# Column sums of the key features from one operand of 128 partitions: two products instead of four, moved behind the first down tile

## The chip, the cores and the metric

One core of a Trainium2 chip runs the whole program. Its engines work side by side and wait for each other by semaphores: TensorE (PE, matrix products into PSUM), VectorE (DVE), ScalarE (ACT), GpSimd (POOL) and SyncE (SP), whose queue issues nearly all DMAs. Each engine runs its instructions in the order in which they stand in the program. The metric is the time of one execution on the device in microseconds; lower is better. Three runs of the kernel before took 445.38, 446.20 and 446.23 us, the median is 446.2.

## What is computed

`x` is 2048 rows of 512. Part A is a linear attention with 32 heads of 16 columns, part B a dense layer with Mish, and a gate mixes them row by row:

```python
g = _sigmoid((x * gate_w).sum(-1, keepdims=True))
# A: q, k, v of x @ wqkv, by head
phi_q = concat(softmax(q @ w_phi), softmax(-(q @ w_phi)))
phi_k = concat(softmax(k @ w_phi), softmax(-(k @ w_phi)))
kv  = einsum("bhsf,bhsd->bhfd", phi_k, v)
z   = einsum("bhsf->bhf", phi_k)            # sums over all 2048 rows
o   = einsum("bhqf,bhfd->bhqd", phi_q, kv) / (einsum("bhqf,bhf->bhq", phi_q, z) + 1e-6)
a   = o @ wo
b   = mish(x @ w1 + b1) @ w2
out = g * a + (1 - g) * b
```

The change is about `z`: for each of 2 x 512 feature columns one sum over all rows, which is needed on every partition, since every row of `phi_q` is multiplied with it.

## The kernel before

The kernel runs in two parts. Part A goes over eight chunks of 256 rows, two tiles of 128 rows each. For a tile it makes the products for k, v and q, turns k into its two softmaxes (maximum and minimum by head, two subtractions, exponential, sums `S`, reciprocal `rS`, and the scaling `ml`), stores q to DRAM for later (`st`), and adds the tile's features to `zacc` on GpSimd (`z0`, `z1`; L324, 128 partitions by 1024 columns). At the end of every second chunk `kv` multiplies features and v into one PSUM bank. After the last chunk `km` masks and turns that bank, and eight small DMAs put it into `kvb`.

Part B goes over four blocks of 512 rows. A block has eleven `up` tiles (`up0` to `up10`, 12 products with w1 each, called U0, U1, ... in the prediction), each followed by `mi` (Mish on ScalarE), `hi` (its high half, ScalarE), `lo` (the rest, GpSimd), and eleven `dn` (down) steps, each with the products of one such tile with w2 into four PSUM banks. `gr` (ScalarE and SP, L560) copies the one row of `up0` that holds the gate's argument out of PSUM, sends it to DRAM, and reads it back by rows. `hc` and `cd` deal with a leftover of the first tile. In between the attention of the block is worked off: `lq` loads q again, `mx`, `mn`, `d0`, `d1`, `E`, `S`, `rS` make its features as in part A, `T` multiplies them with the sums `zb`, `D`, `m`, `de`, `rd` and `sc` make the divisor, `es` scales, `tr` transposes on VectorE and stores to DRAM (`ed`), `mv` reads it back turned (`eT`), `nu` multiplies it with `kvb` (`num`), `oh` and `ol` split the result, `wo` multiplies with wo, and `fi` stores the output. The numeral behind a step is its tile; a `+` behind it means the next block's, a `'` the previous chunk's.

Every float32 product is made from parts: a value is split into a high part in a reduced format (`float32r`) and the rest, and three products (high by high, high by rest, rest by high) are added. So is `z`: `zh` (L459) makes the high part of `zacc` on ScalarE, `zl` (L485) the rest on VectorE, and `z` (L476) multiplies a matrix of ones with both, for each half of the columns: four products. A product with ones sums over the 128 partitions and leaves the sum on all of them. Two activations bring the results into `zb`.

The order of all steps is written out by hand in the texts FIRST to BLOCK. Each word runs the function of that name, and every instruction is pinned, so that each engine keeps the order of the text; what the engines do at the same time follows from their waits. LAST is the last chunk of part A, BLOCK0 the first block of part B.

PSUM has eight banks: three take turns for the `up` tiles and for the k and q products of part A (tag `a`), four for the v products and the down sums (tag `dn`), and one is for `kvp` (tag `kv`), later used by `num` and `wo`. A tile that takes a bank over has to wait until the last reader of the tile before it is done. In SBUF two buffers of 1024 columns (tag `tx`) hold x of a chunk as loaded, then the parts of `zacc`, then `T`. wo is loaded in two pieces (`ldo0`, `ldo1`); `WH0` and `WH1` make their high parts on ScalarE, `WL0` and `WL1` the rest on GpSimd (L446).

Almost all matrix products are recorded on L100 and all activations on L120, which are helpers; the tile's name tells them apart.

Of the kernel before, what the change touches and what calls it, by code (L numbers as in the profile page):

```python
# [9 lines left out]
F32R = mybir.dt.float32r  # L10
# [42 lines left out]
"""  # L53
LAST = """
    k0 mx0 mn0 d00 d10 k1 E0 XH0 mx1 mn1 d01 d11 wx E1 v0 S0 rS0 ml0 z0 ve0 XH1 S1 rS1 ml1 z1 XL0 XL1
    v1 ve1 lq2+ mx1+ mn1+ d01+ d11+ q0 qe0 st0 q1 zh qe1 st1 E1+ zl kv' kv S0+ rS0+ km
"""

BLOCK0 = """
    up0 mi0 hi0 lo0 gr lq3 ldo0 ldo1 S1 rS1 mx2 mn2 up1 @z mi1 hi1 lo1 hc T0 D0 m0 de0 rd0 sc0 es0 tr0 up2 mi2 hi2 lo2 dn0
    T1 D1 m1 de1 rd1 sc1 es1 tr1 mv0 lq0+ lq1+ d02 d12 mx3 mn3 d03 d13 up3 mi3 hi3 lo3 WH0 dn1
    up4 mi4 hi4 lo4 WH1 WL0 dn2 E2 S2 T2 rS2 D2 m2 de2 rd2 sc2 es2 tr2 up5 mi5 hi5 lo5 WL1 dn3 E3 ge gg up6 mi6 hi6 lo6 dn4
    up7 mi7 hi7 lo7 dn5 S3 T3 rS3 D3 m3 de3 rd3 sc3 es3 tr3 mv1 up8 mi8 hi8 lo8 dn6
    mx0+ mn0+ d00+ d10+ mx1+ mn1+ d01+ d11+ lq2+ lq3+ up9 mi9 hi9 lo9 dn7 E0+ E1+ S0+ T0+ LX0 rS0+ D0+ m0+ de0+ rd0+ sc0+
    up10 mi10 hi10 lo10 dn8 dn9 cd nu0 nu1 oh0 ol0 es0+ tr0+ XH0+ XL0+ S1+ T1+ rS1+ LX1 df0 df1 wo0 ag0 wo1 oh1 ol1 ag1 D1+ fi0
    m1+ de1+ rd1+ sc1+ df2 df3 wo2 ag2 fi1 XH1+ XL1+ es1+ fi2 wo3 ag3 fi3 tr1+ mv0+
"""
# [19 lines left out]
def tile_gated_mix(ctx: ExitStack, tc: tile.TileContext, xT, wv, wkT, wqT, bd, w1a, w1b, b1, w2a, w2b, wo, out):  # L89
# [6 lines left out]
    pin = tc.keep_in_program_order  # L96
    V, G_, A_, Sy = nc.vector, nc.gpsimd, nc.scalar, nc.sync

    def mm(*a, **k):
        return pin(nc.tensor.matmul(*a, **k))  # L100

    def T(shape, dt, tag, bufs, name):
        nm[0] += 1
        return sp.tile(shape, dt, name=f"{name}_{nm[0]}", tag=tag, bufs=bufs)
# [4 lines left out]
    def k4(name, tag, dt=F32):  # L109
        return T([P, 1024], dt, tag, {"tx": 2, "oh": 2, "z": 1}[tag], name)  # L110

    def k2(name, tag, dt=F32):
        return T([P, 512], dt, tag, {"pq": 3, "io": 4, "hl": 8}[tag], name)

    def psum(name, tag, bufs={"a": 3, "dn": 4, "kv": 1}):
        nm[0] += 1
        return pp.tile([P, 512], F32, name=f"{name}_{nm[0]}", tag=tag, bufs=bufs[tag])

    def act(out_, in_, fn=AF.Copy, **k):
        return pin(A_.activation(out_, in_, fn, **k))  # L120
# [7 lines left out]
    def f32(ap):  # L128
        return ap.bitcast(F32)
# [48 lines left out]
    onr = T([P, P], F32R, "hc", 1, "onr")  # L178
# [20 lines left out]
    def at(key, name, fn):  # L199
        steps.setdefault((key, name), []).append(fn)  # L200
# [12 lines left out]
    zacc = k4("zacc", "z")  # L213
# [240 lines left out]
    B = {}  # L454

    def mid_ops():
        key = ("A", NCH - 1)

        def zh():  # L459
            B["zs"] = [k4("zs", "tx", F32R) for _ in range(2)]  # L460
            act(B["zs"][0], zacc)

        def km():

            B["km"] = k2("km", "io")
            m = B["km"][:, :256]
            pin(V.tensor_mul(m.rearrange("p (n x) -> p n x", x=32), kvs[0].rearrange("p g (a x) -> p (g a) x", a=2), mask[:, None, :].to_broadcast([P, 8, 32])))
            pin(V.transpose(m, m))
            m = m.rearrange("p (g a x) -> p g a x", g=NG, a=2)
            for e in range(2):  # L470
                for r in range(2):
                    for a in range(2):
                        o, i = 64 * r + 32 * a, 64 * e + 32 * r
                        pin(Sy.dma_start(kvb[o : o + 32, e::2, :], m[i : i + 32, :, a, :]))

        def z():  # L476
            B["zb"] = k4("zb", "z")
            for a in range(2):
                ps = psum("z", "dn")
                for j in range(2):  # L480
                    mm(ps, onr, B["zs"][j][:, a * 512 : (a + 1) * 512], start=(j == 0), stop=(j == 1))
                act(B["zb"][:, a * 512 : (a + 1) * 512], ps)

        at(key, "zh", zh)
        at(key, "zl", lambda: pin(V.tensor_sub(B["zs"][1], zacc, f32(B["zs"][0]))))  # L485
        at(key, "km", km)
        at(("B", 0), "@z", z)


# [219 lines left out]
    wo_ops()  # L709
    w2_ops(("A", NCH - 1))  # L710
    mid_ops()
    for b in range(NB):
        b_ops(b)
# [155 lines left out]
```

## Time and profile before

| | |
|---|---|
| median of three runs | 446.2 us (445.38 to 446.23) |
| the profiled execution | 445.59 us |
| its span, first to last instruction | 443.7 us |
| granted TensorE clock, mean | 1.000 |
| part A on TensorE | up to about 149.8 us of the span |
| first block of part B | from about 149.8 us on |

The profile is of one execution. Its times count from the start of the span, and the 1.9 us between 443.7 and 445.59 lie around it. In a row of a timeline stand the start, the duration, the engine, the line, the operation, the tiles written and read, their shapes, how many instructions are merged in the row, and in brackets how long the engine was idle before and who released it. A duration of a TensorE row is longer than the time until the next one starts, as products overlap; the distance of starts counts. Rows of waits have the engine that waits, who releases it, the sum, the number of waits and the longest one. Rows of DMA issues have tiles, the queue, how many, the KB of each and the median time to landing.

### The profile page before, as it was taken

Reading aid. Unit: us, or ns where it says so; the run is one execution under the profiler, and the core shown is the slowest. Engines: PE = TensorE matmul, PEld = TensorE weight load, DVE = VectorE, ACT = ScalarE, POOL = GpSimd, SP = SyncE. Lnnn points to the kernel's source line nnn. Section 1 sums busy time; section 2 is a strip of 40 time slices with the busy share of each in tenths; the row PEclk is TensorE's granted clock in tenths of the full one; section 3 lists DMA queues with packets and bytes.
Section 4 is the critical chain, followed back from the end, with each engine's and each line's share of the span. In section 5 each row is a group of like instructions: output and inputs, shape, how many; then the busy total and the mean of one; then the engine's idle time right before and its main releaser. Section 6 shows DMA issues by size and latency. Waiting matters only on the chain.

```text
span 443.7 us, 7192 instructions
## 1 busy us (share of the span) xinstructions
PE 439.0 (99%) x2878; PEld 360.5 (81%) x2878; DVE 310.0 (70%) x414; ACT 203.8 (46%) x290; POOL 160.9 (36%) x100
## 2 busy tenths in 40 slices
PE   8999999999999999999999999999999999999997
PEld 7888888888888888887888878888878888887885
DVE  3987658459399999999999898369679329601103
ACT  3644433444335384836366442646352645342331
POOL 3078686676862344621023120214310222411121
PEclk9999999999999999999999999999999999999999
DMA  7721622614504126326353524322505302320002
GB/s 264 283 96 47 193 79 87 193 13 176 189 27 120 49 46 220 103 97 189 120 195 113 148 95 139 94 96 95 191 0 184 102 1 95 118 72 1 1 0 95
DMA packets 28809, 49.11 MB, mean 111 GB/s; under 512 B 6244, under 2 KB 14948, under 8 KB 28776
## 3 DMA queue, kind: packets, MB, share of 16 engines
q1 hardware_dynamic: 28456, 48.26, 33.6%
q8 instruction: 22, 0.36, 0.4%
q10 hardware_dynamic: 288, 0.39, 0.3%
q14 instruction: 11, 0.09, 0.1%
q0 software_dynamic: 32, 0.01, 0.0%
HBM read 31.21 MB, written 16.79 MB: 108 GB/s over the span
## 4 chain that ended last, share of the span: by engine, by line
PE 98%; DMA 1%; SPq 0%; DVE 0%; issue 0%
PE proj L100 30%; PE up L100 27%; PE down L100 26%; PE wo L100 10%; PE kvp L100 2%; PE num L100 2%; DMA wT<-in_wkT_dram 1%; PE fuse L100 1%; PE rest L100 0%; PE z L100 0%; DVE io L687 0%; SPq L156 0%; SPq L148 0%
## 5 line engine op out<-in xcount | busy, mean ns | idle before, releaser
L521 POOL TENSOR_TENSOR l<-act,h 128x512 fp32r<-128x512 f32 (+1 forms) x44 | 63.4, 1442 | 217.4 <-ACT h L120 190.8
L120 ACT ACTIVATE act<-up,b1s 128x512 f32<-128x512 f32 x44 | 30.3, 688 | 78.2 <-PE up L100 77.8
L324 POOL TENSOR_TENSOR zacc<-zacc,E 128x1024 f32<-128x1024 f32 x16 | 39.7, 2484 | 38.6 <-DVE E L286 38.6
L120 ACT ACTIVATE E<-E 128x1024 f32<-128x1024 f32 x32 | 33.6, 1061 | 41.5 <-DVE E L271 41.5
L286 DVE TENSOR_TENSOR E<-E,Sm 128x1024 f32<-128x1024 f32 x32 | 46.1, 1442 | 1.0
L100 PE MATMUL wo<-woh,ohl 128*128 128x512 f32 x128 | 41.2, 389 | 0.0
L275 DVE TENSOR_REDUCE Sm<-E 128x64 f32<-128x1024 f32 x32 | 38.5, 1204 | 0.0
L100 PE MATMUL down<-w2ah,h 128*128 128x512 f32 x96 | 37.6, 392 | 0.0
L256 DVE TENSOR_REDUCE mx<-proj 128x32 f32<-128x512 f32 x16 | 11.0, 690 | 31.4 <-PE proj L100 31.4
L100 PE MATMUL down<-w2al,h 128*128 128x512 f32 x80 | 31.2, 390 | 0.0
L100 PE MATMUL down<-w2ah,l 128*128 128x512 f32 x80 | 31.1, 389 | 0.0
L120 ACT ACTIVATE h<-act 128x512 fp32r<-128x512 f32 (+2 forms) x48 | 30.3, 632 | 1.5
L422 DVE TENSOR_TENSOR xbl<-xraw,xbh 128x1024 fp32r<-128x1024 f32 x8 | 12.0, 1528 | 26.8 <-ACT xbh L120 26.8
L100 PE MATMUL down<-w2bh,h 128*128 128x512 f32 x78 | 30.6, 392 | 0.0
L100 PE MATMUL down<-w2bl,h 128*128 128x512 f32 x78 | 30.4, 389 | 0.0
L100 PE MATMUL down<-w2bh,l 128*128 128x512 f32 x78 | 30.4, 389 | 0.0
L100 PEld LDWEIGHTS wo<-woh,ohl 128*128 128x128 f32 x128 | 24.0, 188 | 5.0
L120 ACT ACTIVATE io<-wo,g_sb 128x512 f32<-128x512 f32 x16 | 11.0, 690 | 36.1 <-PE wo L100 36.1
L120 ACT ACT_TABLE_LOAD x19 | 24.4, 1283 | 3.5 <-PE up L100 3.2
L100 PE MATMUL up<-xbh,w1ah 128*128 128x512 f32 x96 | 25.8, 390 | 0.0
L100 PE MATMUL up<-xbh,w1al 128*128 128x512 f32 x96 | 25.7, 389 | 0.0
L100 PE MATMUL up<-xbl,w1ah 128*128 128x512 f32 x96 | 25.7, 389 | 0.0
(126 smaller groups left out, 977.5 us busy)
## 6 DMA issues: line engine op xcount, KB each, us to landing
ed<-E SPq DMA_DIRECT2D x16, 512.0 KB, 2.9
eT<-ed SPq DMA_DIRECT2D x64, 128.0 KB, 3.3
xraw<-in_xT_dram SPq DMA_DIRECT2D x15, 512.0 KB, 5.0
pqd<-qs SPq DMA_DIRECT2D x16, 256.0 KB, 2.7
pq<-pqd SPq DMA_DIRECT2D x16, 256.0 KB, 3.9
out_dram<-io SPq DMA_DIRECT2D x15, 256.0 KB, 2.0
raw<-in_w1a_dram SPq DMA_DIRECT2D x3, 512.0 KB, 5.5
raw<-in_w2a_dram SPq DMA_DIRECT2D x3, 512.0 KB, 4.1
```

Of the source, the lines that this page charges most:

```text
L100: return pin(nc.tensor.matmul(*a, **k))
L120: return pin(A_.activation(out_, in_, fn, **k))
L256: pin(V.tensor_reduce(d[name], hv(src()), axis=AX.X, op=op))
L275: pin(V.tensor_reduce(d["S"], hv(d["E"][:, :]), axis=AX.X, op=ALU.add))
L286: pin(eng.tensor_mul(hv(d["E"][:, :]), hv(d["E"][:, :]), d["S"][:, :, None].to_broadcast([P, 2 * H, DH])))
L324: at(key, f"z{t}", lambda d=d: pin(G_.tensor_add(zacc, zacc, d["E"])))
L422: pin(V.tensor_sub(xb[b][1][:, :, sl], kt(raw[h], SC), f32(xb[b][0][:, :, sl])))
L521: pin(G_.tensor_sub(U[i]["l"][:n, :], U[i]["a"][:n, :], f32(U[i]["h"][:n, :])))
```

## The change

`z` is made otherwise. The upper 64 partitions of `zacc` are copied to the lower ones by a DMA (`zd`), GpSimd adds the two halves (`zf`), and the high part (`zh`, now 64 partitions) and the rest (`zl`, written to the upper 64 partitions) stand in one tile `zs` of 128 partitions. So one product with ones adds both parts and all partitions, two products in all. `zd` and `zf` stand in LAST where `zh` and `zl` were; these two are now in BLOCK0, `zh` ahead of `gr` and `zl` behind `S1 rS1`. `z` itself moves behind `dn0`, which in turn has `up2` and `up3` ahead of it, and its results are in the banks of the tags `kv` and `a` instead of `dn`. Some steps of the attention in BLOCK0 (`d02 d12 mx3`) go ahead of `T0`, and `WL0` and `WL1` move back behind `lo8` and `lo9`.

```diff
 LAST = """
...
-    v1 ve1 lq2+ mx1+ mn1+ d01+ d11+ q0 qe0 st0 q1 zh qe1 st1 E1+ zl kv' kv S0+ rS0+ km
+    v1 ve1 lq2+ mx1+ mn1+ d01+ d11+ q0 qe0 st0 q1 zd qe1 st1 E1+ zf kv' kv S0+ rS0+ km
 """
...
 BLOCK0 = """
-    up0 mi0 hi0 lo0 gr lq3 ldo0 ldo1 S1 rS1 mx2 mn2 up1 @z mi1 hi1 lo1 hc T0 D0 m0 de0 rd0 sc0 es0 tr0 up2 mi2 hi2 lo2 dn0
-    T1 D1 m1 de1 rd1 sc1 es1 tr1 mv0 lq0+ lq1+ d02 d12 mx3 mn3 d03 d13 up3 mi3 hi3 lo3 WH0 dn1
-    up4 mi4 hi4 lo4 WH1 WL0 dn2 E2 S2 T2 rS2 D2 m2 de2 rd2 sc2 es2 tr2 up5 mi5 hi5 lo5 WL1 dn3 E3 ge gg up6 mi6 hi6 lo6 dn4
-    up7 mi7 hi7 lo7 dn5 S3 T3 rS3 D3 m3 de3 rd3 sc3 es3 tr3 mv1 up8 mi8 hi8 lo8 dn6
-    mx0+ mn0+ d00+ d10+ mx1+ mn1+ d01+ d11+ lq2+ lq3+ up9 mi9 hi9 lo9 dn7 E0+ E1+ S0+ T0+ LX0 rS0+ D0+ m0+ de0+ rd0+ sc0+
+    up0 mi0 hi0 lo0 @zh gr lq3 ldo0 ldo1 S1 rS1 @zl mx2 mn2 up1 mi1 hi1 lo1 d02 d12 mx3 up2 mi2 hi2 up3 dn0 @z hc lo2 mi3 hi3 lo3
+    T0 D0 m0 de0 rd0 sc0 es0 tr0 T1 D1 m1 de1 rd1 sc1 es1 tr1 mv0 lq0+ lq1+ mn3 d03 d13 WH0 dn1
+    up4 mi4 hi4 lo4 WH1 dn2 E2 S2 T2 rS2 D2 m2 de2 rd2 sc2 es2 tr2 up5 mi5 hi5 lo5 dn3 E3 ge gg up6 mi6 hi6 lo6 dn4
+    up7 mi7 hi7 lo7 dn5 S3 T3 rS3 D3 m3 de3 rd3 sc3 es3 tr3 mv1 up8 mi8 hi8 lo8 WL0 dn6
+    mx0+ mn0+ d00+ d10+ mx1+ mn1+ d01+ d11+ lq2+ lq3+ up9 mi9 hi9 lo9 WL1 dn7 E0+ E1+ S0+ T0+ LX0 rS0+ D0+ m0+ de0+ rd0+ sc0+
...
+        def zd():
+            B["zt"] = k4("zt", "tx")
+            pin(Sy.dma_start(B["zt"][:64, :], zacc[64:, :]))
+
         def zh():
-            B["zs"] = [k4("zs", "tx", F32R) for _ in range(2)]
-            act(B["zs"][0], zacc)
+            B["zs"] = k4("zs", "tx", F32R)
+            act(B["zs"][:64, :], zacc[:64, :])
...
             for a in range(2):
-                ps = psum("z", "dn")
-                for j in range(2):
-                    mm(ps, onr, B["zs"][j][:, a * 512 : (a + 1) * 512], start=(j == 0), stop=(j == 1))
+                ps = psum("z", ("kv", "a")[a])
+                mm(ps, onr, B["zs"][:, a * 512 : (a + 1) * 512], start=True, stop=True)
                 act(B["zb"][:, a * 512 : (a + 1) * 512], ps)
...
-        at(key, "zh", zh)
-        at(key, "zl", lambda: pin(V.tensor_sub(B["zs"][1], zacc, f32(B["zs"][0]))))
+        at(key, "zd", zd)
+        at(key, "zf", lambda: pin(G_.tensor_add(zacc[:64, :], zacc[:64, :], B["zt"][:64, :])))
+        at(("B", 0), "@zh", zh)
+        at(("B", 0), "@zl", lambda: pin(V.tensor_sub(B["zs"][64:, :], zacc[:64, :], f32(B["zs"][:64, :]))))
```

## The prediction

> **What bounds the kernel now.** Read first were the page's busy times, its chain of work and TensorE's own waits.
>
> ```profile
> span 443.7 us, 7192 instructions
> PE 439.0 (99%) x2878; PEld 360.5 (81%) x2878; DVE 310.0 (70%) x414; ACT 203.8 (46%) x290; POOL 160.9 (36%) x100
> ...
> PE 98%; DMA 1%; SPq 0%; DVE 0%; issue 0%
> ```
>
> ```profile
> PE warm L100 <- DVE ones L170: 1.1, 1, 1.1
> PE fuse L100 <- DMA bds<-in_bd_dram: 0.3, 1, 0.3
> PE fuse L100 <- DMA wT<-in_wkT_dram: 0.2, 1, 0.2
> ```
>
> TensorE is busy for 439.0 of 443.7 us, the chain is 98% TensorE, and these three rows, all from the start, are every wait that it has. So the other engines are hidden with some slack each, a product removed is worth its own time, and a wait put on TensorE is paid in full: nothing behind it gives it back. The edit lies at the step from part A to part B, so its timeline on TensorE came next.
>
> ```profile
> 149.79 1.20 PE L100 MATMUL up<-xbh,w1ah 128*128 128x512 f32 x4
> ...
> 152.64 1.07 PE L100 MATMUL up<-xbh,w1ah 128*128 128x512 f32 x4
> ...
> 155.36 1.07 PE L100 MATMUL z<-zs,onr 128*128 128x512 f32 x4
> 156.27 1.07 PE L100 MATMUL up<-xbh,w1ah 128*128 128x512 f32 x4
> ```
>
> These are the first tiles of products with w1, U0 to U2 (U3, the fourth, comes behind the first down products): each of 12 products takes 2.72 us (152.64 to 155.36), the four z products 0.91 us (155.36 to 156.27).
>
> **What is removed.** Two of four z products: 0.91 / 2 = 0.45 us off TensorE. That is all the change can win there, 0.10% of 446.2 us. The full-width zs on ScalarE and its remainder on VectorE go too; neither is on TensorE's path.
>
> **What is moved on TensorE: the price of the change.** The order becomes U0, U1, U2, U3, dn0, z, dn1. With neither z nor dn0 ahead of it, U3 could start two tiles after U1's start: 152.64 + 2 x 2.72 = 158.08. But U tiles take turns in three PSUM buffers (tag "a"), and in the built program U3 gets U0's. It must wait for ScalarE to have read U0 twice: mish, and gr, which copies the gate's row. gr is now behind zs on ScalarE, in a strict order.
>
> ```profile
> 149.62 1.06 ACT L120 ACTIVATE zs<-zacc 128x1024 fp32r<-128x1024 f32 x1 [3.71 <-POOL zacc L324]
> ...
> 153.09 1.06 ACT L120 ACTIVATE E<-E 128x1024 f32<-128x1024 f32 x1 [1.93 <-DVE E L271]
> 154.17 1.28 ACT L120 ACT_TABLE_LOAD   x1
> 155.47 0.69 ACT L120 ACTIVATE act<-up,b1s 128x512 f32<-128x512 f32 x1
> 156.19 1.29 ACT L120 ACTIVATE h<-act 96x512 fp32r<-96x512 f32 x2
> 157.50 0.63 ACT L120 ACTIVATE l<-act 32x512 fp32r<-32x512 f32 x1
> 158.15 0.59 ACT L120 ACTIVATE gr<-up 1x512 f32<-1x512 f32 x1
> 158.76 1.09 ACT L120 ACTIVATE zb<-z 128x512 f32<-128x512 f32 x2
> ```
>
> ScalarE's chain starts at 153.09 with the exponential, whose releaser is VectorE, and runs gapless through the table load to gr. Before, gr ended at 158.74, and z, U2 and dn0 kept TensorE busy until U3. Now zs starts where gr did, 158.15. Its price at 64 partitions is in no row; the bounds are 0.63 (half of its elements, like l) and 1.06 (as before). Rows of 96 and of 32 partitions take the same 0.63 to 0.65 (two in 1.29, one in 0.63), so partitions don't count and I take 1.06. gr then runs from 159.23 to 159.82. U3 is held from 158.08 to 159.82, 1.74, with the handing over about 1.8 us; with the lower bound 1.3.
>
> **What is added, and what hides it.** zd copies zacc's upper 64 partitions to the lower ones (256 KB); GpSimd adds them (zf); zs and its remainder (zl) make one 128-partition operand.
>
> ```profile
> 142.72 2.40 POOL L324 TENSOR_TENSOR zacc<-zacc,E 128x1024 f32<-128x1024 f32 x1 [8.80 <-DVE E L286]
> 146.37 3.22 POOL L324 TENSOR_TENSOR zacc<-zacc,E 128x1024 f32<-128x1024 f32 x1 [1.25 <-DVE E L286]
> 156.89 1.29 POOL L521 TENSOR_TENSOR l<-act,h 96x512 fp32r<-96x512 f32 x1 [7.31 <-ACT h L120]
> ```
>
> zacc is whole at 146.37 + 3.22 = 149.59; zd can go then. Behind it on SP wait only the store of the last q tile, read in the last block, and the copies to kvb, not due before 155. zf costs between 1.29 (512 elements) and 2.40 (1024); it has 1024, so 2.40. GpSimd was idle for 7.31 us before 156.89, so zf is hidden if the copy lands by 154.5. zl (1.21 at most) is due when z starts, after dn0 at 159.9 + 2.72 + 1.81 = 164.4, with zs done at 159.2: covered by 4 us. z's two results go to the kv buffer, read by km's mask before 156.2, and to U1's, free by then.
>
> ```profile
> w2x<-w2ah SPq DMA_DIRECT2D x1, 192.0 KB, 3.1
> w2al<-w2al SPq DMA_DIRECT2D x3, 64.0 KB, 2.0
> ```
>
> ```profile
> pqd<-qs SPq DMA_DIRECT2D x1, 256.0 KB, 2.0
> ```
>
> zd's landing is the one cost that matters and no row has it. Copies within SBUF of 64 and 192 KB take 2.0 and 3.1 us: 256 KB on that line 3.7. A store of 256 KB to DRAM took 2.0 between 150 and 152 (third row), so the bounds are 2.0 and 3.7. I take about 3.2, nearer to copies of its own kind: landing 152.8. The Trainium skill's "SBUF — State Buffer", section "Door 1: The DMA port swizzle", says that 64 partitions reach no more DMA ports than 32, half of what 128 reach. By its 196 to 218 GB/s the data would take an estimated 1.2 to 1.3 us instead of 0.6; the trace agrees in kind, as the 32-partition copy takes 2.0 with a quarter of the store's bytes.
>
> wo's two subtractions on GpSimd go from behind the fifth and sixth lo to behind the ninth and tenth, about 195 and 200. The first wo product comes at 210.97: 8 us of cover. hc and the fourth tile's mish move behind zb, about 165; that tile's down products come after U4 and dn2.
>
> ```profile
> 159.88 1.23 DVE L589 TENSOR_TENSOR T<-E,zb 128x1024 f32<-128x1024 f32 x1 [0.40 <-ACT zb L120]
> ...
> 173.10 0.72 DVE L269 TENSOR_TENSOR E<-pq,mx 128x512 f32<-128x512 f32 x1
> 173.74 2.88 DVE L271 TENSOR_TENSOR E<-mn,pq 128x512 f32<-128x512 f32 x1
> 176.55 0.67 DVE L256 TENSOR_REDUCE mx<-pq 128x32 f32<-128x512 f32 x1
> ...
> 196.01 1.25 DVE L604 STREAM_TRANSPOSE E<-E 128x1024 f32<-128x1024 f32 x1
> ```
>
> What else is late is VectorE's chain behind zb. T, at 159.88 before, now stands behind d02, d12 and mx3. zb ends about 166.0 (164.4 + 0.45 + 1.09); mx3 needs the fourth q tile:
>
> ```profile
> 163.75 0.49 SPq L585 DMA_DIRECT2D pq<-pqd  x1
> ...
> 197.69 4.29 SPq L627 DMA_DIRECT2D eT<-ed  x8
> ```
>
> ```profile
> pq<-pqd SPq DMA_DIRECT2D x16, 256.0 KB, 3.9
> ```
>
> km comes 1.1 earlier without the old zl, so this load is issued at 162.6, lands at 166.5, and T starts at 167.2: 7.3 late. The three moved operations, 173.10 to 177.14 before, give back 4.0. The fourth tile's transpose (196.01) is 3.3 late.
>
> ```profile
> 207.57 1.96 PE L100 MATMUL num<-eT,kvb 64*32 64x256 f32 x64
> DMA to landing us min/median/max: 2.6/3.3/6.0
> ```
>
> The last eT copy is issued at 201.98 + 3.3 = 205.3 and lands, at the median 3.3, at 208.6. Its half of num stood at 207.57 + 0.98 = 208.55 and comes 1.35 later, 209.9. So 1.3 us of slack is left: I cost it at nothing, at the maximum 6.0 it is 1.4 us.
>
> **The sum.** -0.45 + 1.8 = +1.35 us. On the profiled execution (443.7 span, 445.59 in all) that is 446.9, on the median of the runs shown (446.2) 447.6. The profiled one and the three runs (445.38 to 446.23) have the mean 445.85; from there it is 447.2, which I forecast.
>
> **Rivals.** (a) GpSimd gets in ahead of VectorE: slower.
>
> ```profile
> 151.78 0.67 DVE L269 TENSOR_TENSOR E<-pq,mx 128x512 f32<-128x512 f32 x1
> 152.38 0.68 DVE L271 TENSOR_TENSOR E<-mn,pq 128x512 f32<-128x512 f32 x1
> ```
>
> ```profile
> 130.99 2.93 POOL L324 TENSOR_TENSOR zacc<-zacc,E 128x1024 f32<-128x1024 f32 x1
> ```
>
> ```profile
> 130.99 0.67 DVE L269 TENSOR_TENSOR E<-pq,mx 128x512 f32<-128x512 f32 x1
> 131.59 2.88 DVE L271 TENSOR_TENSOR E<-mn,pq 128x512 f32<-128x512 f32 x1
> ```
>
> At 131 a GpSimd sum that came during d0 ran between d0 and d1, and d1 took 2.88 instead of 0.68. The same pair stands at 151.78 and 152.38, and its d1 releases the exponential that starts ScalarE's chain. If zf is ready before 152.38, that is, if zd lands within 2.7 us of 149.6, everything down to gr slips by 2.2 and the wait becomes 4.0: 445.85 - 0.45 + 4.0 = 449.4. The store's 2.0 speaks for it, the two copies' line against. By the Trainium skill's "DMA: Bandwidth & Descriptors", section "Anatomy of one DMA — SWDGE (gpsimd) path", a DMA takes 2.0 us plus its bytes at 436 GB/s, here an estimated 2.6, just on this side; the page gives it for GpSimd's own queue, and zd goes through SP's.
>
> (b) The eT landing of 6.0, or a wo subtraction holding one of the fourth tile's VectorE operations for its 2.4 us, uses up the 1.3 us: +1.4 on the forecast, 448.6.
>
> ```profile
> 146.12 4.54 DVE L422 TENSOR_TENSOR xbl<-xraw,xbh 128x1024 fp32r<-128x1024 f32 x2
> ```
>
> (c) Not slower: VectorE's two xbl subtractions, 4.54 together because the zacc of 146.37 ran between them, both go ahead of it. Then d1, and ScalarE's chain, come about 2.1 earlier, gr ends at 157.7, ahead of 158.08, and only -0.45 is left: 445.4. From 1.74 earlier on there is no wait. Against it: nothing ahead of 149.6 changes order on either engine.
>
> **How the numbers follow.** Forecast 0.62, (a) 0.17, (b) 0.14, (c) 0.05, anything else 0.02. The forecast's own range is 446.4 (zs at 0.63, the profiled base) to 447.7 (median base). With (b) and most of (a) it is 446.4 to 449.7. About 0.2% (0.9 us) can be told from no change; a gain of that size is out of reach at 0.45, so faster has 0.02. Same takes (c) and the low end of the forecast: 0.11. Slower 0.87.
>
> **What would show it.** Right: one new wait of TensorE, up on ScalarE's gr, of 1.8 us with U3 starting near 159.9; zs between l and gr; zf starting at about 153, after VectorE's d1 of 0.68. For (a): d1 stretched to about 2.9, U3 near 162. For (b): a num or down product waiting on a DMA near 210. Wrong: no wait at U3, or a landing of zd past 155.7, where zs itself would be late.

## The result and the profile after

The changed kernel takes 448.02 us (median of 6 executions, 447.78 to 449.56), the kernel before beside it 445.86 (445.38 to 446.36): a ratio of 1.0054, 95% interval 1.0039 to 1.0068. It is slower by 2.2 us; the forecast was 447.2 and a loss of 1.35 on the profiled execution. The profiled execution of the changed kernel took 447.78 with a span of 446.1 (before: 445.59 and 443.7), with the granted clock at 1.0 in both.

TensorE's waits in the changed kernel (total us, times, longest):

```profile
PE up L100 <- ACT gr L120: 1.6, 1, 1.6
PE warm L100 <- DVE ones L170: 1.1, 1, 1.1
PE fuse L100 <- DMA bds<-in_bd_dram: 0.4, 1, 0.4
PE fuse L100 <- DMA wT<-in_wkT_dram: 0.2, 1, 0.2
PE down L100 <- POOL l L527: 0.2, 1, 0.2
```

Two rows are new: the first, which was forecast, and the last, which was not. Their places on TensorE's timeline (start, length, what ran, and in brackets the idle time before it and its releaser):

```profile
149.69 1.20 PE L100 MATMUL up<-xbh,w1ah 128*128 128x512 f32 x4
...
159.77 1.19 PE L100 MATMUL up<-xbh,w1ah 128*128 128x512 f32 x4 [1.62 <-ACT gr L120]
...
162.63 0.39 PE L100 MATMUL down<-w2ah,h 128*128 128x512 f32 x1
...
164.44 0.61 PE L100 MATMUL z<-zs,onr 128*128 128x512 f32 x2
164.89 0.39 PE L100 MATMUL down<-w2ah,h 128*128 128x512 f32 x1
...
211.17 0.39 PE L100 MATMUL down<-w2bl,h 128*128 128x512 f32 x1
211.76 0.50 PE L100 MATMUL down<-w2bh,l 128*128 128x512 f32 x1 [0.20 <-POOL l L527]
...
212.56 0.40 PE L100 MATMUL down<-w2bh,l 128*128 128x512 f32 x1
213.06 0.50 PE L100 MATMUL wo<-woh,ohl 128*128 128x512 f32 x1
213.40 0.40 PE L100 MATMUL wo<-wol,ohl 128*128 128x512 f32 x1
```

U3 starts at 159.77. Without a wait it would have started two tiles after U1 (152.55 + 5.44 = 157.99): 1.78 us. The two z products take 0.45 (164.44 to 164.89). Near 211 the products should follow each other at 0.23 us; the steps 211.17 to 211.76, 212.56 to 213.06 and the first step behind each (0.34) are 0.36, 0.27 and twice 0.11 too long: 0.85 us.

The measure used below is the stretch from the start of U0 to the start of the last product: 149.79 to 440.31 before, 149.69 to 442.55 after, 290.52 against 292.86 us. It is longer by 2.34, and it leaves out the start of the program and its end. U3 itself takes 2.86 us to the next product (159.77 to 162.63) where U1 takes 2.72, so its standstill costs 0.14 more. The parts then add up: -0.45 + 1.78 + 0.14 + 0.85 = 2.32.

### The profile page after: what moved, and what is told of

Same layout as the page of the kernel before. It is cut to its first block, busy times and chain, and to the rows that moved or that the text cites. A ratio compares the mean times of both kernels' runs of the same rounds, so it can differ in the third digit from the quotient of the medians.

```text
span 446.1 us, 7186 instructions
## 1 busy us (share of the span) xinstructions
PE 439.2 (98%) x2876; PEld 359.6 (81%) x2876; DVE 311.3 (70%) x414; ACT 204.0 (46%) x290; POOL 161.0 (36%) x101
## 4 chain that ended last, share of the span: by engine, by line
PE 81%; DVE 14%; DMA 2%; issue 1%; SPq 1%; ACT 0%; DVEq 0%
PE proj L100 27%; PE up L100 20%; PE down L100 20%; PE wo L100 10%; DVE Sm L275 2%; DVE E L286 1%; DVE den L603 1%; PE kvp L100 1%; DVE T L595 1%; DVE Dn L599 1%; PE num L100 1%; DMA wT<-in_wkT_dram 1%; DVE xbl L422 1%; DVE E L269 1%; PE fuse L100 1%
## 5 line engine op out<-in xcount | busy, mean ns | idle before, releaser
L527 POOL TENSOR_TENSOR l<-act,h 128x512 fp32r<-128x512 f32 (+1 forms) x44 | 61.6, 1400 | 215.6 <-ACT h L120 194.5
L286 DVE TENSOR_TENSOR E<-E,Sm 128x1024 f32<-128x1024 f32 x32 | 45.0, 1406 | 1.0
```

The source lines that it names most:

```text
L286: pin(eng.tensor_mul(hv(d["E"][:, :]), hv(d["E"][:, :]), d["S"][:, :, None].to_broadcast([P, 2 * H, DH])))
L527: pin(G_.tensor_sub(U[i]["l"][:n, :], U[i]["a"][:n, :], f32(U[i]["h"][:n, :])))
```

## The experiments

Each run's time is a median, and its ratio to the kernel before on the same chip has its 95% interval. U0 and the stretch come from the profiled execution. e9 to e11 were made on one chip to repeat what the runs ahead of them had left doubtful.

| kernel | us | ratio to before | U0 at | stretch |
|---|---|---|---|---|
| before | 445.86 to 446.49 | 1 | 149.79 | 290.52 |
| the change | 448.02 | 1.0054 [1.0039, 1.0068] | 149.69 | 292.86 |
| the change again (e9) | 447.85 | 1.0042 [1.0026, 1.0058] | 149.70 | 292.82 |
| e1, gr ahead of zs | 447.24 | 1.0026 [1.0015, 1.0038] | 149.78 | 291.72 |
| e2, U3 behind dn0 | 446.31 | 1.0006 [0.9997, 1.0015] | 149.92 | 291.01 |
| e3, wo's subtractions early | 448.21 | 1.0049 [1.0036, 1.0061] | 149.74 | 292.50 |
| e4, before with them late | 445.96 | 1.0002 [0.9992, 1.0011] | 149.74 | 290.52 |
| e5, them on VectorE | 448.01 | 1.0041 [1.0028, 1.0053] | 150.20 | 292.00 |
| e5 again (e10) | 447.74 | 1.0034 [1.0022, 1.0047] | 150.15 | 292.00 |
| e6, e2 and e5 together | 445.77 | 0.9994 [0.9985, 1.0003] | 150.10 | 290.20 |
| e6 again (e11) | 445.90 | 0.9987 [0.9977, 0.9998] | 150.05 | 290.20 |
| e7, short copy | 447.81 | 1.0046 [1.0030, 1.0062] | 149.71 | 292.82 |
| e8, d02 d12 mx3 put back | 449.01 | 1.0068 [1.0053, 1.0083] | 149.75 | 293.37 |
| e12, order alone | 445.68 | 0.9991 [0.9981, 1.0001] | 150.25 | 290.19 |

**e1: is it gr that holds U3?**

```
-    up0 mi0 hi0 lo0 @zh gr lq3 ...
+    up0 mi0 hi0 lo0 gr @zh lq3 ...
```

> The changed kernel with one edit: ScalarE copies the gate's row (gr) ahead of zs instead of behind it. Theory 1, U3 waits for gr because gr stands behind zs: gr starts at 158.05 and ends near 158.7, U3 could start at 157.99, so its wait falls from 1.78 to about 0.7 and the kernel to about 447.0 us (1.06, the length of zs, under the changed kernel's 448.0; still 1.1 over before). z stays covered, since zs then ends at 159.8 and its remainder near 161.0, ahead of z. Rival, U3 waits for something else that happens to end near 159.7 (the copy's sums, or mish of a later tile): the wait stays at 1.6 to 1.8 and the time at 448.0.

TensorE's and ScalarE's rows of e1:

```profile
158.77 1.19 PE L100 MATMUL up<-xbh,w1ah 128*128 128x512 f32 x4 [0.54 <-ACT gr L120]
```

```profile
158.12 0.59 ACT L120 ACTIVATE gr<-up 1x512 f32<-1x512 f32 x1
158.74 1.06 ACT L120 ACTIVATE zs<-zacc 64x1024 fp32r<-64x1024 f32 x1
```

gr ends at 158.71 and U3 starts 0.06 later. The stretch is 1.14 us shorter than the change's. The wait follows gr; theory 1 holds, and so does the price of zs, 1.06.

**e2: U3 behind the first down products.**

```
-    ... up2 mi2 hi2 up3 dn0 @z hc lo2 ...
+    ... up2 mi2 hi2 dn0 up3 @z hc lo2 ...
```

> The changed kernel with one edit: U3 and the first down products change places on TensorE, so U3 starts about 1.8 us later by the order, at 159.8, when gr ends (159.7). Theory 1: no wait of up at all, 1.8 us under the changed kernel, 446.2 us, if the second loss (0.85 us near 211) is VectorE's own lateness, which does not depend on U3's wait. Rival, the second loss is only an echo of the 1.8 us stall: both go, 445.4. Rival, the bank is not what holds U3: 448.0 as the changed kernel.

The wait of up is gone from e2's list; the other one is still there:

```profile
PE warm L100 <- DVE ones L170: 1.1, 1, 1.1
PE down L100 <- POOL l L527: 0.2, 1, 0.2
```

The stretch falls by 1.85 and 446.31 stands beside the 446.2 of theory 1. The second loss is no echo of the first. zb ended about 1.6 us earlier here, and VectorE's T still started at 166.3, as mx3 ahead of it waited for the fourth q tile; at d11+ VectorE was still 2.2 us behind the kernel before (204.23 against 202.06):

```profile
165.71 0.69 DVE L256 TENSOR_REDUCE mx<-pq 128x32 f32<-128x512 f32 x1 [0.76 <-DMA pq<-pqd]
166.31 1.22 DVE L595 TENSOR_TENSOR T<-E,zb 128x1024 f32<-128x1024 f32 x1
```

**What the second loss is.** Read back from the late l in the changed kernel, first on GpSimd, then ScalarE, then VectorE:

```profile
195.08 2.40 POOL L446 TENSOR_TENSOR wol<-raw,woh 128x1024 fp32r<-128x1024 f32 x1
...
200.55 2.41 POOL L446 TENSOR_TENSOR wol<-raw,woh 128x1024 fp32r<-128x1024 f32 x1
210.39 1.31 POOL L527 TENSOR_TENSOR l<-act,h 128x512 fp32r<-128x512 f32 x1 [7.44 <-ACT h L120]
```

```profile
206.53 1.06 ACT L120 ACTIVATE E<-E 128x1024 f32<-128x1024 f32 x1 [1.33 <-DVE E L271]
207.62 1.28 ACT L120 ACT_TABLE_LOAD   x1
208.91 0.69 ACT L120 ACTIVATE act<-up,b1s 128x512 f32<-128x512 f32 x1
```

```profile
195.24 2.29 DVE L603 SCALAR_TENSOR_TENSOR den<-Dn 128x32 f32<-128x32 f32 x1
...
199.47 1.25 DVE L610 STREAM_TRANSPOSE E<-E 128x1024 f32<-128x1024 f32 x1
...
201.79 1.72 DVE L269 TENSOR_TENSOR E<-pq,mx 128x512 f32<-128x512 f32 x1
...
205.82 0.68 DVE L271 TENSOR_TENSOR E<-mn,pq 128x512 f32<-128x512 f32 x1
...
210.60 1.16 DVE L603 SCALAR_TENSOR_TENSOR den<-Dn 128x32 f32<-128x32 f32 x1
...
212.32 1.28 DVE L653 TENSOR_TENSOR ohl<-num,ohl 128x512 fp32r<-128x512 f32 x2
```

The same places in the kernel before, on GpSimd, TensorE and VectorE:

```profile
206.63 1.31 POOL L521 TENSOR_TENSOR l<-act,h 128x512 fp32r<-128x512 f32 x1 [7.43 <-ACT h L120]
```

```profile
210.04 0.40 PE L100 MATMUL down<-w2bh,l 128*128 128x512 f32 x1
```

```profile
202.06 0.68 DVE L271 TENSOR_TENSOR E<-mn,pq 128x512 f32<-128x512 f32 x1
...
209.46 1.29 DVE L647 TENSOR_TENSOR ohl<-num,ohl 128x512 fp32r<-128x512 f32 x2 [0.82 <-ACT ohl L120]
```

l of the eleventh tile waits for h, mish and the table load, these for the exponentials of the next block's first two q tiles (E0+ and E1+), which stand ahead in ScalarE's order, and E1+ for VectorE's d11+. Before, that l ended at 207.94 and its product ran at 210.04, 2.1 us of slack; now it ends at 211.70, and its product could have run at 211.40. wo behind it waits for ol0 (ohl, 212.32; 209.46 before), whose reading frees the bank of num that the first wo product writes: the first of its two subtractions takes 0.68 and ends at 213.00, and wo starts at 213.06.

ol0 is tied to l as well. den, shortly ahead of it on VectorE, started at 210.60 while GpSimd made that l, took 1.16 instead of 0.19, and ended 0.06 behind it. In all seven profiles in which wo waits (the change, e9, e1, e2, e3, e7, e8) ol0 starts 0.61 to 0.62 behind the end of l, and wo 0.05 to 0.06 behind ol0's first subtraction. So it is wo's wait that sets the loss, and down's wait for l lies within it. The repetition of the change (e9, below) shows it: num took longer there (2.25 us to the next product, 1.89 above; the profile doesn't name what it waited for), down had no wait, and wo started as late as here:

```profile
208.96 2.32 PE L100 MATMUL num<-eT,kvb 64*32 64x256 f32 x64
...
213.07 0.50 PE L100 MATMUL wo<-woh,ohl 128*128 128x512 f32 x1
```

VectorE had been held by both wol before that: den, which takes 0.19 by itself, ended with GpSimd's first wol at 197.5, and d0 of 0.68 ran out 0.55 behind the second. By the Trainium skill's "SBUF — State Buffer", section "Who interferes with whom", a VectorE instruction with two inputs in SBUF shares a port with a GpSimd instruction that reads SBUF, and the one that comes second waits; the trace agrees, with 2.29 for 0.19.

**e3 and e4: the place of wo's two subtractions**, moved in the change (e3) and in the kernel before (e4).

```
e3, on the change:
-    up4 mi4 hi4 lo4 WH1 dn2 ... lo5 dn3 ... lo8 WL0 dn6 ... lo9 WL1 dn7
+    up4 mi4 hi4 lo4 WH1 WL0 dn2 ... lo5 WL1 dn3 ... lo8 dn6 ... lo9 dn7
e4, on the kernel before:
-    up4 mi4 hi4 lo4 WH1 WL0 dn2 ... lo5 WL1 dn3 ... lo8 dn6 ... lo9 dn7
+    up4 mi4 hi4 lo4 WH1 dn2 ... lo5 dn3 ... lo8 WL0 dn6 ... lo9 WL1 dn7
```

> The changed kernel with wo's two subtractions on GpSimd put back to where they stood before (behind the fifth and the sixth lo). Theory 2, the loss near 211 is VectorE's whole lateness, part of it from z standing later and part from GpSimd's subtractions holding it, and the new place of the subtractions is the cheaper one: at the old place they held VectorE for 2.2 us (2.88 for 0.68 at 173.74) and 1.8 us (2.03 for 0.23 at 182.85), at the new one for 2.1 and about 1.0, so the fourth tile's transpose comes 1 to 2 us later still, num waits for its eT copies near 210, and the time rises by 1 to 2 us, to 449 to 450. Rival, the late place alone makes the second loss: it goes, 0.85 us under the changed kernel, 447.2.

> The kernel before with nothing but wo's two subtractions moved to where the change puts them (behind the ninth and the tenth lo). Theory 2: VectorE gains about 4.0 us between 173 and 186 and loses about 3 near 194 to 203, so the tenth lo comes no later than before and no wait arises: 445.9, as before. Rival, the late place alone makes the second loss: VectorE and with it the tenth lo come about 3 us later against the 2.1 us of slack that lo had before (it ended at 207.94, its product ran at 210.04), a wait of about 1 us, 446.9 or more.

VectorE and GpSimd in e3:

```profile
175.69 1.06 DVE L618 TENSOR_TENSOR Dn<-Dn,Sm 128x64 f32<-128x64 f32 x1
...
180.65 2.40 DVE L269 TENSOR_TENSOR E<-pq,mx 128x512 f32<-128x512 f32 x1
...
200.23 1.25 DVE L610 STREAM_TRANSPOSE E<-E 128x1024 f32<-128x1024 f32 x1
...
205.54 0.69 DVE L271 TENSOR_TENSOR E<-mn,pq 128x512 f32<-128x512 f32 x1
```

```profile
173.27 3.41 POOL L446 TENSOR_TENSOR wol<-raw,woh 128x1024 fp32r<-128x1024 f32 x1
...
180.10 2.40 POOL L446 TENSOR_TENSOR wol<-raw,woh 128x1024 fp32r<-128x1024 f32 x1
...
210.12 1.31 POOL L527 TENSOR_TENSOR l<-act,h 128x512 fp32r<-128x512 f32 x1 [8.78 <-ACT h L120]
```

e3 met neither number. The fourth tile's transpose is 0.76 later than in the change, d11+ 0.28 earlier, l 0.27 earlier; the stretch shrank by 0.36 and the time didn't move (448.21). Theory 2's 1 to 2 us had carried over the holds of the kernel before, but the old place meets other VectorE work in the new order: holds of 0.8 (175.69, where 0.23 is the usual length) and 1.7 (180.65), where 2.2 and 1.8 were counted. e4 came out as theory 2 said: 445.96, the same stretch to the hundredth, though d1 was held for 2.88 there:

```profile
199.62 2.88 DVE L271 TENSOR_TENSOR E<-mn,pq 128x512 f32<-128x512 f32 x1
```

So the late place does not make the loss by itself, and the early place would not have saved it.

**e5 and e10: the two subtractions on VectorE**, at the same places of the order.

```
-            pin(G_.tensor_sub(wob["l"][:, sl], raw[j], f32(wob["h"][:, sl])))
+            pin(V.tensor_sub(wob["l"][:, sl], raw[j], f32(wob["h"][:, sl])))
```

> The changed kernel with wo's two subtractions done by VectorE instead of GpSimd, at the same places of the order. Theory 2, the loss near 211 is VectorE's lateness, to which GpSimd's two subtractions add by holding it (den 2.29 us for 0.19 at 195.24, d0 1.72 for 0.68 at 201.79): both holds go, and the second subtraction, 1.2 us on VectorE, stands behind the exponentials' input, so the eleventh tile's chain on ScalarE and GpSimd comes 1.5 to 2 us earlier than in the changed kernel. The wait of down on GpSimd's l and that of wo behind it go, the wait of up stays at 1.6 to 1.8: 0.85 us under the changed kernel, 447.2. Rival, VectorE is late from z's place alone and the holds don't matter: both waits near 211 stay, 448.0, or more, since VectorE has 2.4 us of work added.

VectorE and GpSimd in e10:

```profile
195.70 0.19 DVE L603 SCALAR_TENSOR_TENSOR den<-Dn 128x32 f32<-128x32 f32 x1
...
204.28 0.68 DVE L271 TENSOR_TENSOR E<-mn,pq 128x512 f32<-128x512 f32 x1
204.88 1.22 DVE L446 TENSOR_TENSOR wol<-raw,woh 128x1024 fp32r<-128x1024 f32 x1
```

```profile
208.85 1.28 POOL L527 TENSOR_TENSOR l<-act,h 128x512 fp32r<-128x512 f32 x1 [7.51 <-ACT h L120]
```

den takes 0.19 again, d11+ and l come 1.5 us earlier, and both waits near 211 are gone. The stretch is 0.86 shorter, in both executions. Its time, though, is 448.01, not 447.2. In the first run U0 began at 150.20. Both kernels were run once more on one chip, to tell whether that was chance.

> The changed kernel unedited, on the same chip as the next two, since the start of an execution (the 20 warm-up products took 3.86 to 4.64 us, and U0 began at 149.70 to 150.20 us) has differed by up to 0.5 us between the profiled executions and the edits are worth less than 1. If the times shown so far hold: 2.2 us over the kernel before, and from U0's start to the last product 292.9 us.

> wo's two subtractions on VectorE once more, beside the changed kernel on one chip. If the 0.86 us that the stretch from U0 to the last product lost in the first run of this edit (292.00 against 292.86) is real and the late U0 (150.20) was chance: 0.85 us under the changed kernel of this call, and the stretch 292.0. If the edit itself delays the start: U0 again near 150.2, the time again within 0.3 us of the changed kernel.

The late start came again: 150.15 (the change: 149.70). And from the last product's start to the end of the span e10 takes 4.0 us (442.14 to 446.1), the change 3.5. The DMA view of e10's last 6.5 us has a row that the change's lacks:

```profile
q14 instruction: 1, 0.01, 0.4%
```

So the edit wins 0.82 to 0.86 in the stretch that it was meant for, and 0.44 at the start and 0.4 at the end are lost; the measured difference from the change is 0.1 us. The late end belongs to the edit: all four executions with these subtractions on VectorE (e5, e6, e10, e11) take 4.0 us there, the other ten 3.4 to 3.5. The late start is not shown to belong to it. From the first projection product to U0 all fourteen profiles take 142.7 to 142.8 us, so what differs lies in the first 7.5 us, where nothing was edited. There the 20 warm-up products took 3.88 us in the change, where their step falls from 0.21 to 0.11 us at about 4 us, and 4.64 in e10, where it stays at 0.21. Why the pace rises later in some executions is open.

**e6 and e11: both repairs**, the diffs of e2 and e5 in one kernel.

> Both repairs together: U3 behind the first down products and wo's two subtractions on VectorE. If theories 1 and 2 account for all of the loss, TensorE has no wait left behind the start and only the gain of two z products is seen: 0.45 us under the kernel before, ratio 0.9990, 445.6 against 446.1. If a part of the loss is still unnamed, or a wait comes up elsewhere, the time stays at or over that of before, 446.1 to 446.5.

> Both repairs once more: U3 behind the first down products and wo's two subtractions on VectorE. If the first run's stretch of 290.20 us (before: 290.52) is what counts and its late U0 (150.10) was chance: 0.3 to 0.45 us under the kernel before, ratio 0.9990 to 0.9993, and 2.6 us under the changed kernel of this call. If the start is late again: no difference from before, ratio 1.000.

No wait of up or down is left. The stretch is 290.20 in both, 0.32 under before: what the two products fewer are worth is 0.45, and 0.13 comes back in small gaps in dn0 and U3. The times are 0.9994 and 0.9987 of before, but the program as a whole gains nothing: the median span, over the executions of each, is 444.0 and 444.2 us, and 444.0 and 443.9 for the kernel before beside them. What is shorter is the time around the span (1.8 and 1.7 against 2.1 and 2.2), and no row of a profile lies there.

**e7: rival (a) of the prediction, an early landing.** zd and zf take 16 partitions; 48 of the upper 64 are left out of z.

```
-            pin(Sy.dma_start(B["zt"][:64, :], zacc[64:, :]))
+            pin(Sy.dma_start(B["zt"][:16, :], zacc[64:80, :]))
-        ... pin(G_.tensor_add(zacc[:64, :], zacc[:64, :], B["zt"][:64, :]))
+        ... pin(G_.tensor_add(zacc[:16, :], zacc[:16, :], B["zt"][:16, :]))
```

> The changed kernel with a short copy: zd and zf take 16 of the 64 partitions, so 48 partitions of zacc's upper half are left out of z. Rival (a) of the prediction, an early landing lets GpSimd in ahead of VectorE's d1: a copy of 64 KB lands after about 2.0 us instead of 3.6, at 151.6, zf starts before 152.3 and d1 takes about 2.9 instead of 0.68; everything on ScalarE down to gr slips by 2.2 and the wait of up grows from 1.6 to about 3.8: 450.2. The other reading, that GpSimd does not hold VectorE here, or that a sum of 16 partitions is short, or that the small copy does not land earlier: the wait of up stays at 1.6 to 2.1 and the time at 448.0 to 448.5.

The copy's landing in the change, then e7's landing and rows of GpSimd and VectorE:

```profile
DMA to landing us min/median/max: 3.5/3.5/3.5
```

```profile
DMA to landing us min/median/max: 2.8/2.8/2.8
```

```profile
152.47 2.76 POOL L489 TENSOR_TENSOR zacc<-zacc,zt 16x1024 f32<-16x1024 f32 x1 [2.96 <-DMA zt<-zacc]
```

```profile
152.30 0.68 DVE L271 TENSOR_TENSOR E<-mn,pq 128x512 f32<-128x512 f32 x1
```

A quarter of the bytes lands only 0.7 us earlier, and zf misses d1's start by 0.17 us. d1 keeps its 0.68, and zf pays: 2.76 instead of 2.39. The time stays. It shows the border of rival (a) from the far side only; a zf ahead of d1 was not produced, so its 2.2 us stays argued from the pair at 131. One thing beside the copy changed as well: the store of the last q tile, issued 0.57 behind it, took 3.6 us in the change and 2.0 in the kernel before. How much of the copy's 3.5 comes from what runs beside it was not tried.

**e8: the three moved VectorE operations put back.**

```
-    ... up1 mi1 hi1 lo1 d02 d12 mx3 up2 ... mv0 lq0+ lq1+ mn3 d03 d13 WH0 dn1
+    ... up1 mi1 hi1 lo1 up2 ... mv0 lq0+ lq1+ d02 d12 mx3 mn3 d03 d13 WH0 dn1
```

> The changed kernel with d02, d12 and mx3 put back behind the third tile's loads of q, where they stood before. By the prediction they give VectorE 4.0 us back by standing where it would wait for z's copy: undone, T still starts near 166 with the copy of z and the tiles behind it come up to 4 us later, so the loss near 211 grows from 0.85 to 3 or 4 us: 450 to 452. Rival, most of those 4.0 us were time in which GpSimd held VectorE (2.88 us of them were one d1 of 0.68), and their work is 2.0: the fourth tile's transpose comes up to 0.6 us later and the time rises by no more than that, 448.0 to 448.6.

```profile
200.11 1.25 DVE L610 STREAM_TRANSPOSE E<-E 128x1024 f32<-128x1024 f32 x1
```

The transpose comes 0.64 later than in the change, not 4.0, and the stretch grows by 0.51; the time is 1.0 to 1.2 over the change's. The profiled execution was the fastest of its five (448.36), so about half of that is not in the trace. The rival's mechanism fits the trace, though its 448.6 was 0.4 short: 2.2 of the 4.0 us were one d1 of 0.68 held by GpSimd, which is not held where e8 puts it.

**e12: the order alone**, nothing added and nothing moved to another engine.

```
-    ... hi2 up3 dn0 @z ...
+    ... hi2 dn0 up3 @z ...
-    ... dn7 E0+ E1+ S0+ T0+ LX0 rS0+ D0+ m0+ de0+ rd0+ sc0+
-    up10 mi10 hi10 lo10 dn8 dn9 cd nu0 nu1 oh0 ol0 es0+ ...
+    ... dn7 up10 mi10 hi10 lo10 E0+ E1+ S0+ T0+ LX0 rS0+ D0+
+    dn8 dn9 cd nu0 nu1 oh0 ol0 m0+ de0+ rd0+ sc0+ es0+ ...
```

> The changed kernel with the order alone edited, no instruction added or given to another engine: U3 behind the first down products; the eleventh tile's products with w1 and its mish, h and l (up10 to lo10) ahead of the next block's two exponentials on ScalarE, so that its l no longer waits for VectorE; VectorE's ol0, which frees the bank of the first wo product, ahead of the small operations on Dn and den. If the two chains named so far (gr behind zs; VectorE late, so that l and ol0 come late) are the whole loss: no wait of TensorE behind the start, the stretch from U0 to the last product 290.2 us as with wo on VectorE (before: 290.5), and, if U0 starts at 149.7 to 149.9 as in the kernels that gave VectorE nothing to do, a time 0.3 to 0.45 us under before, ratio 0.9990 to 0.9993. Rival, VectorE's lateness only shows further on (num, the second wo product, the next block's first tiles): a wait of 0.3 us or more there, and a time at or over that of before.

GpSimd's eleventh l and VectorE's ol0 in e12:

```profile
203.47 1.29 POOL L527 TENSOR_TENSOR l<-act,h 128x512 fp32r<-128x512 f32 x1 [1.75 <-issue]
```

```profile
209.63 1.27 DVE L653 TENSOR_TENSOR ohl<-num,ohl 128x512 fp32r<-128x512 f32 x2
```

With mish ahead of the exponentials, l ends at 204.76, some 5 us before its product, ol0 comes within 0.2 us of where it stood before the change, and TensorE's only wait left in the list is the one for ones at the start. The stretch is 290.19. VectorE is still late (its d11+ starts at 205.23, 202.06 before); it no longer stands in the way. U0 started late here too (150.25), with no VectorE instruction added. 445.68 is the lowest median of all, 0.9991 [0.9981, 1.0001] of before. The median span is 0.2 shorter (443.65 against 443.85), the stretch 0.33: the loss is gone, but a gain over the kernel before can't be told from no change by the time alone.

## Why the prediction was right, point by point

- **Two products removed, -0.45.** Right: 0.45 from 164.44 to 164.89; net of small gaps 0.32 in the stretch (e6, e12 against before).
- **U3 held by gr, 1.8.** Right in place, cause and size: zs took 1.06, gr ended at 159.72, U3 started at 159.77 (forecast 159.9), 1.78 late. The stretch of e5 against e6 gives 1.80. The sum lacked the 0.14 that U3 loses besides, behind the standstill. e1 moved gr and the wait went with it.
- **zd, zf and zl hidden.** Right. zd landed after 3.5 (taken: 3.2, bounds 2.0 and 3.7), near the upper bound; zf took 2.39 and started at 153.19, behind d1 of 0.68; z at 164.44 had no wait.
- **T 7.3 late, 4.0 given back, the transpose 3.3 late.** The end is right (199.47, 3.46 late), the way to it is not. T came at 166.11, 6.2 late, as the q tile landed after 3.0 and not 3.9. VectorE had nearly caught up by 189 (the third tile's transpose at 188.51 against 188.06), since wo's subtractions no longer held it; then they held it at 195 and 201. e8 shows that the three moved operations themselves are worth 0.6.
- **The step that failed: "So 1.3 us of slack is left: I cost it at nothing".** One reading in it was off: 201.98 is the end of a row of eight copies, the last of them was issued at 201.5, so the slack was 1.8 by the prediction's own terms. In the profiled execution num did not wait. But num was not the next thing due. d11+, E1+, the table load, mish, h and l of the eleventh tile had 2.1 us of slack before and 3.5 with TensorE 1.4 later, and VectorE was 3.8 late there (205.82 + 0.68 = 206.50 against 202.74). This late l held den, den held up ol0, and ol0 the first wo product, at a cost of 0.86. "8 us of cover" for wo's subtractions was true of the wo products and left out what they hold on VectorE.
- **Rival (b)** named that hold ("holding one of the fourth tile's VectorE operations") and put it at 1.4 and at num's copies. It happened, to den and to d0 behind it, at 0.86, and through ScalarE's order and ol0 instead of a DMA. Its other arm, a late eT copy, did not occur in the change; in e3 and e8 such copies landed after 4.3 and 4.7 us, and num's weight loads went on 0.21 behind these landings, within the wait that wo had anyway. It needs both lateness of z and the holds: with the holds alone (e4) or with z's lateness alone (e5, e10) TensorE does not wait near 211.
- **Rival (a)** did not occur: the landing was 3.5 where 2.7 was its limit; whether zf would hold d1 was not tried. By the Trainium skill's "DMA: Bandwidth & Descriptors", section "Anatomy of one DMA — SWDGE (gpsimd) path", the estimate had been 2.6; the trace does not agree for SP's queue at this place, where even 64 KB took 2.8. **Rival (c)** did not occur either; xbl and zacc kept their order.

The forecast of 447.2 was 0.8 low, as the sum lacked the second loss of 0.86 and the 0.14. 448.02 lies above the forecast's own range, whose upper end comes to 447.55 by its terms (446.2 - 0.45 + 1.8) and not to 447.7; only the wider range with rival (b) covers it. So the direction and the first wait were right for the reason given, and of the measured loss more than a third was not in the sum.

## What to carry to other kernels

When one engine is busy all the time, price a moved operation by the buffer it releases: zs was hidden itself, and still cost 1.06 us because the read behind it held a PSUM bank. When an engine off the path becomes late, list everything that is next due from it, also through another engine's order (here exponential, table load, mish), and not only the one consumer with a DMA. A strict order can decouple this for nothing: work that does not need the late engine goes ahead of work that does (e12).

## What the runs showed of the hardware that was not expected

- A sum of GpSimd over 16 partitions and 1024 elements took 2.76 with some 0.4 of waiting in it, over 64 partitions 2.39, over 128 partitions 2.40 to 2.41, and l over 128 partitions and 512 elements 1.31: in these rows partitions don't count, elements per partition do. ScalarE's zs agrees, 1.06 at 64 and at 128 partitions.
- A copy within SBUF took 2.8 us for 64 KB and 3.5 for 256 KB at the same place, beside a store: most of it did not go by the bytes. The copies of 64 KB near 137 took 2.0.
- GpSimd can hold VectorE for several times the length of VectorE's instruction: den of 0.19 took 2.29 beside a wol and 1.16 beside an l.
- The start of the program differed by up to 0.56 us between kernels whose first 140 us were not edited (U0 at 149.69 to 150.25), and came out the same within 0.06 us where a kernel was profiled twice (149.69 and 149.70, 150.20 and 150.15, 150.10 and 150.05). The last pair got there by different ways: e6's warm-up products took 4.63 us, e11's 3.84 with a wait of 0.80 for a load behind them. Edits worth less than that are better read from the stretch that they touch.
